# Steps of the triangular inverses moved from VectorE to GpSimd, with a newly planned instruction order

## The chip, the cores and the metric

The kernel runs on one core of one Trainium2 chip. The metric is device time in microseconds (us) for one execution, the median of several. Engines are named as in the profile: PE (TensorE, matmuls; its weight loads are PEld), DVE (VectorE), ACT (ScalarE), POOL (GpSimd), SP (SyncE, which here only issues DMAs).

## What is computed

A linear recurrence over 768 steps for 32 heads (4 batches of 8), and then two dense layers on its output, 3072 tokens of width 320, hidden width 2048:

```
for t in range(S):                                   # S = 768
    y[:, :, t] = einsum('bhd,bhde->bhe', r_t, state)
    Sa = einsum('bhde,bhe->bhd', state, a_t)
    state = state * w_t - outer(Sa, b_t) + outer(v_t, k_t)
...
h = x @ w_in;   x = (h * tanh(softplus(h))) @ w_out          # layer 1
h = x @ w_in2;  x = (h * cos(h)) @ w_out2                    # layer 2
```

All inputs are float32 (the layers' weights are float64 and are split into high and low parts on the chip).

## The kernel before

**The recurrence** is cut into chunks of 32 steps, and the heads into two halves of 16: 2 x 24 = 48 chunks, numbered g = 0 to 47, one after another. Inside a chunk the steps are solved at once with the inverse of a unit triangular matrix of 32 x 32 per head. Each chunk has two parts.

- `pre(g)` needs no state and runs up to seven chunks ahead: two scans on DVE (L570 and L576, tiles PE and RP), four multiplications on DVE (L584 to AM, L590 to KB), two memsets of AM on POOL (L598), the matrices of the chunk on PE (L607), four masked evacuations on DVE (L617, back into AM), transposes (L640). A DMA (L630, L631) writes the triangular part of AM to DRAM (`l_d`).
- `chain(g)` carries the state and so sets the order of chunks: matmuls L782, L805, L796, L854, and two groups L880 at its end, with evacuations between them on ACT (L390, L788) and DVE (L864 to FR, L891 to SV, L899 to Y), and transposes L924 for the next chunk.

**The inverse.** Two chunks form a batch; there are 24, bt = 0 to 23. `inverse(bt)` loads the 2 x 16 matrices' two diagonal blocks of 16 x 16 from `l_d` into tile XM (64 partitions), and inverts them by forward substitution: 14 times a multiplication into XT (L679) and an addition into XM (L677), each on the result of the one before it, 28 steps in all, on 14 to 56 elements per partition. Both inputs of a step lie in SBUF. Then a short memset sets the diagonal (L686), a DMA stores XM to DRAM (`t_d`, L690), another loads it in a new layout to TT (L694), and `halves` joins the blocks: a transpose on DVE (L721), matmuls L716, an operation on DVE (L724), matmuls L718, a copy. TT is what L805 and L796 of the chunk multiply with.

**The dense layers.** Weights are converted on ACT, DVE (L466, L471, L479) and POOL (L508, low parts wil, wol, wix, read from staging tiles H, AU, RL). Layer 1 takes blocks of 256 tokens as the recurrence finishes them: matmuls L983 (16 for each of 8 parts of the hidden width), Mish on ACT (L1053, L1055), the low part of the result on DVE (L1058, tile GL), matmuls L964 (12 for each part). Layer 2 follows when layer 1 is done (L998, L1014, and L983 and L964 for two small blocks), with its low parts on POOL (L1142). There are 1792 matmuls L983 and 1344 L964 in all.

**What sets the order.** Every operation is a task with an engine, a duration in us, predecessors and the buffers it takes. `Plan.run` is a greedy planner: it keeps a clock per engine, starts next the task that can start earliest (small differences are decided by priorities), and writes the instructions in that order. Tasks with `port=True` on DVE and POOL are never planned at the same time. On the chip each engine works off its instructions in the planned order, whatever the real durations are, and waits for semaphores. PE puts matmuls of layer 1 into places where the chain isn't ready. The priorities put the chain first, then `pre` and `inverse` by chunk, then the dense layers.

Of the kernel before, what the change touches and what calls it, by code (L numbers as in the profile page):

```python
# [14 lines left out]
ALU = mybir.AluOpType  # L15
# [23 lines left out]
def bc(ap, shape):  # L39
    return ap.to_broadcast(list(shape))  # L40
# [43 lines left out]
MODE = {"pre.g1": "128x64", "chain.rvz": "128x64", "chain.fmm.f": "128x64", "chain.rhs": "128x32",  # L84
        "chain.zmm": "32x32", "halves.mm.f": "32x32", "chain.stm": "64x128", "chain.ztm": "full"}
LEAVE, CHANGE, ENTER = 0.22, 0.12, 0.13
AGE = 8.0
WAIT = 8.0
SP_SAFE = 1.0

# [161 lines left out]
def body(ctx, tc, ins, out):  # L252
# [141 lines left out]
    def pa(key):  # L394
        return bank[P.at(key)]

    def dve(n, passes=1.0):
        return 0.065 + 0.00104 * n * passes

    def act(n, psum=True, ptr=0):  # L400
        return (0.05 if psum else 0.093) + 0.000833 * n + 0.093 * ptr

    def pool(n):
        return 0.1 + 0.0022 * n
# [7 lines left out]
    INV_LEAD = 32  # L412
    AHEAD_W = 6
    DIRECT = 48
    HV_D, HV_P = (0.36, 0.41), 0.5
    B_HI2 = 1.0
    am_on, GLE = lambda g, d: ("DVE", 0.33), ("DVE",)
    HIE = EITHER
    HIE2, HID2 = ("DVE",), (0.34,)
    LOE2, LOD2 = ("POOL", "DVE"), (pool(512), dve(512))  # L420
# [125 lines left out]
    def fifo(name, t):  # L546
        p = prev_fifo.get(name)
        if p is not None:
            t.preds.append(p)
        prev_fifo[name] = t  # L550
        return t

    def pre(g):
# [16 lines left out]
            V.tensor_tensor_scan(out=pe().rearrange("p q t -> p (q t)"), data0=INv()[:, 768:1032],  # L570
                                 data1=D1.rearrange("p q t -> p (q t)"), initial=0.0, op0=ALU.mult, op1=ALU.add)

        t_sc = fifo("scan", P.add("DVE", 0.62, scan, preds=[t_ld, S_D], acq=[("PE", k("PE"))], prio=pr, port=True))
        def rscan():
            V.reciprocal(out=D1R[:, :, C:], in_=pe()[:, :, C:])
            V.tensor_tensor_scan(out=rp().rearrange("p q t -> p (q t)")[:, ::-1], data0=INv()[:, 769:1033][:, ::-1],  # L576
                                 data1=D1R.rearrange("p q t -> p (q t)")[:, ::-1], initial=0.0,
                                 op0=ALU.mult, op1=ALU.add)

        t_rp = P.add("DVE", 0.85, rscan, preds=[t_sc], acq=[("RP", k("RP"))], prio=pr, port=True)  # L580

        def am_f(p):
            r = slice(64 * p, 64 * p + 40)
# [12 lines left out]
        def az_f(p):  # L596
            r = slice(64 - 64 * p, 128 - 64 * p)
            return lambda: G.memset(am()[r, p], 0.0)  # L598

        t_z0 = P.add("POOL", 0.24, az_f(0), preds=[t_a1], prio=pr)  # L600
        t_z1 = P.add("POOL", 0.24, az_f(1), preds=[t_z0], prio=pr)

        def g1():
            gp = pa(k("G"))[:, 0:256].rearrange("p (q x) -> p q x", x=2 * C)
# [7 lines left out]
        def gev(p, c):  # L612
            r = slice(64 - 64 * p, 128 - 64 * p)

            def f():
                gp = pa(k("G"))[64 * c:64 * c + 64, 0:256].rearrange("r (q p t) -> r p q t", p=2, t=C)
                V.tensor_tensor(out=am()[r, p].rearrange("r (q c) t -> r c q t", c=2)[:, c], in0=gp[:, p],  # L617
                                in1=bc(maskG[r].unsqueeze(1), (64, NQ // 2, C)), op=ALU.mult)
            return f

        t_gl = []
        for c2 in range(2):
            for p in range(2):
                t_gl.append(P.add("DVE", 0.22, gev(p, c2), preds=[t_g], rel=[k("G")], prio=pr))
        Gev[g] = t_gl
        bt, ci = BT_OF[g]
        ld_v = l_d[bt].rearrange("(c q p) j t -> c p j q t", q=NQ, p=2)
# [25 lines left out]
    def inverse(bt):  # L653

        g0, cnt = BATCH[bt]
        pr = -5e3 + (g0 + cnt) * 10 - INV_LEAD
        n = cnt * NU
        rows = lambda: slice(64 * P.at(("X", bt)), 64 * P.at(("X", bt)) + 2 * n)
        x = lambda: XM[rows(), 0:528]
        xu = lambda: XT[rows()]  # L660
        part = lambda h: x()[n * h:n * h + n, 16 - 16 * h:528 - 16 * h]
        blk = lambda: x()[:, 16:528].rearrange("p (j t) -> p j t", t=C)
        dr = lambda d, h: d[bt][:, 16 * h:16 * h + 16].rearrange("n j t -> n (j t)")

        def ld():
            for h in range(2):
                SP.dma_start(part(h), dr(l_d, h))

        t = P.add("SP", 1.0, ld, preds=[ldma[g0 + i] for i in range(cnt)] + [S_X], acq=[("X", ("X", bt))], lat=DMA_LAT, prio=pr)

        def step(i, add):
            w = 15 - i

            def f():
                tv, b = xu()[:, :i * w].rearrange("p (j t) -> p j t", j=i), blk()
                if add:
                    V.tensor_tensor(out=b[:, 0:i, i + 1:16], in0=b[:, 0:i, i + 1:16], in1=tv, op=ALU.add)  # L677
                else:
                    V.tensor_tensor(out=tv, in0=bc(b[:, i:i + 1, i + 1:16], (2 * n, i, w)),  # L679
                                    in1=bc(b[:, 0:i, i:i + 1], (2 * n, i, w)), op=ALU.mult)  # L680
            return f

        for i in range(1, 15):
            for add in range(2):
                t = P.add("DVE", dve(i * (15 - i)), step(i, add), preds=[t], lat=0.13, prio=pr, port=True)
        t = P.add("DVE", 0.1, lambda: V.memset(x()[:, 16:512:33], 1.0), preds=[t], prio=pr)  # L686

        def st():
# [75 lines left out]
    def chain(g):  # L764
# [20 lines left out]
        t = P.add("PE", 0.3, rhs, preds=Gev[g] + [ldma[g], io[g][2]] + (Sev[g - 1] if c else []),  # L785
                  acq=[("PA", k("R"))], rel=[k("AM"), k("SV")], cols=550, prio=pr)
        mated("rhs", c, t)
        t = P.add("ACT", act(160), lambda: A.activation(rs().rearrange("p g d -> p (g d)"), pa(k("R"))[:, 0:160],  # L788
                                                        AF.Copy, scale=-1.0),
                  preds=[t], acq=[("RS", k("RS"))], rel=[k("R")], prio=pr)  # L790

# [80 lines left out]
        ykey = ("Y", hf, yb)

# [456 lines left out]
```

## Time and profile before

| | before |
|---|---|
| median of 3 runs | 1167.32 us (1166.85 to 1177.08) |
| profiled execution | 1172.64 us; its span in the trace is 1170.9 us |
| PE busy | 1047.1 us (89%), 16120 matmul instructions |
| DVE busy | 851.3 us (73%), 2275 instructions |
| ACT busy | 546.0 us (47%) |
| POOL busy | 228.1 us (19%), 278 instructions |
| granted TensorE clock | 0.955 of full speed in the mean |

A float32 matmul of the recurrence appears as two instructions in the trace, so its 16 matmuls of L880 per chunk are 32 there; those of the dense layers appear as one. Times in the trace are counted from the start of the span. Busy PE time is modelled at its ends and overlaps, so it is read together with the counts of matmuls.

### The profile page before, as it was taken

How to read it: one execution, taken by the hardware profiler on the slowest of the kernel's cores; microseconds unless marked ns; L12 is line 12 of the kernel's file. 1: busy time of each engine (PE TensorE's matmuls, PEld its weight loads, DVE VectorE, ACT ScalarE, POOL GpSimd, SP SyncE). 2: the span in 40 equal slices, each digit the busy share in tenths (PEclk: the TensorE clock that was granted, in tenths of full speed). 3: DMA queues.
4: the chain of work that ended last, by engine and by line, in shares of the span. 5: the costliest groups of instructions: out<-in, count | busy, mean ns of one | idle time of the engine just before them, and what ended most of it. 6: DMA issues, size and time to landing. Idle time of an engine off the chain costs nothing. (4 is left out here: it accounts for less than half of the span.)

```text
span 1170.9 us, 39034 instructions
## 1 busy us (share of the span) xinstructions
PE 1047.1 (89%) x16120; PEld 951.9 (81%) x16120; DVE 851.3 (73%) x2275; ACT 546.0 (47%) x1384; POOL 228.1 (19%) x278
## 2 busy tenths in 40 slices
PE   1364988989899988989999999999999999999997
PEld 1353877877787777877888999999999899999997
DVE  8889898879888898788883599433555555555554
ACT  3344464555545555455454444434443444444433
POOL 4223210000000000000000034100333333333333
PEclk9985896989999999999899999999999999999999
DMA  8564345455544555445543354210100000000000
GB/s 236 160 160 144 104 134 156 113 133 142 135 114 129 156 136 156 100 126 134 131 113 89 115 158 138 67 57 26 53 25 1 25 25 26 26 25 12 13 12 23
DMA packets 104913, 112.05 MB, mean 96 GB/s; under 512 B 63520, under 2 KB 84256, under 8 KB 104736
## 3 DMA queue, kind: packets, MB, share of 16 engines
q1 hardware_dynamic: 104736, 109.56, 33.6%
q8 instruction: 127, 2.08, 0.8%
q14 instruction: 50, 0.41, 0.1%
HBM read 91.43 MB, written 18.09 MB: 94 GB/s over the span
## 5 line engine op out<-in xcount | busy, mean ns | idle before, releaser
L1142 POOL TENSOR_TENSOR GL<-H,GH 128x512 fp32r<-128x512 f32 x96 | 124.6, 1298 | 260.6 <-ACT GH L1140 246.4
L390 ACT ACTIVATE FL<-bank 64x160 f32<-64x160 f32 (+1 forms) x376 | 101.7, 295 | 124.3 <-PE bank L924 59.9
L1133 ACT ACTIVATE T<-T,half_pi 128x512 f32<-128x512 f32 x96 | 69.5, 724 | 115.7 <-DVE T L1130 115.7
L1126 DVE TENSOR_SCALAR T<-bank 128x512 f32<-128x512 f32 x96 | 66.4, 692 | 77.6 <-PE bank L998 63.8
L1058 DVE TENSOR_TENSOR GL<-H,GH 128x512 fp32r<-128x512 f32 x96 | 71.4, 744 | 67.6 <-ACT GH L1055 66.6
L1053 ACT ACTIVATE H<-bank 128x512 f32<-128x512 f32 x96 | 57.4, 598 | 119.3 <-PE bank L983 114.4
L1135 DVE TENSOR_TENSOR H<-bank,T 128x512 f32<-128x512 f32 x96 | 66.2, 689 | 56.2 <-ACT T L1133 54.8
L598 POOL MEMSET AM<- 64x256 f32 x96 | 29.4, 306 | 390.9 <-issue 313.3
L607 PE MATMUL bank<-AM,KB 104*64 104x64 f32 x768 | 37.2, 247 | 67.9 <-DVE KB L590 56.9
L983 PE MATMUL bank<-XH,wih 128*128 128x256 f32 x448 | 95.4, 295 | 1.4 <-ACT GH L1055 1.4
L1140 ACT ACTIVATE GH<-H 128x512 fp32r<-128x512 f32 x96 | 60.6, 632 | 72.4 <-DVE H L1135 72.2
L983 PE MATMUL bank<-XL,wih 128*128 128x256 f32 x448 | 91.5, 287 | 0.0
L983 PE MATMUL bank<-XH,wil 128*128 128x256 f32 x448 | 90.5, 284 | 0.4 <-issue 0.4
L607 PEld LDWEIGHTS bank<-AM,KB 104*64 104x64 f32 x768 | 32.0, 158 | 71.2 <-issue 70.3
L880 PE MATMUL bank<-FR,FL 104*64 104x72 f32 x1536 | 72.1, 251 | 16.8 <-issue 8.7
L880 PEld LDWEIGHTS bank<-FR,FL 104*64 104x64 f32 x1536 | 62.8, 155 | 26.1 <-issue 14.6
L983 PEld LDWEIGHTS bank<-XH,wih 128*128 128x128 f32 x448 | 71.0, 194 | 3.4 <-ACT GH L1055 1.5
L679 DVE TENSOR_TENSOR XT<-XM 64x26 f32<-64x26 f32 (+6 forms) x336 | 67.4, 201 | 7.4 <-DMA XM<-l_d 0.3
L677 DVE TENSOR_TENSOR XM<-XM,XT 64x26 f32<-64x26 f32 (+6 forms) x336 | 67.0, 199 | 7.6
L983 PEld LDWEIGHTS bank<-XL,wih 128*128 128x128 f32 x448 | 71.5, 197 | 0.0
L983 PEld LDWEIGHTS bank<-XH,wil 128*128 128x128 f32 x448 | 70.3, 194 | 0.6 <-issue 0.6
L983 PE MATMUL bank<-XH,wix 128*128 128x256 f32 x224 | 69.9, 312 | 0.0
(165 smaller groups left out, 2973.2 us busy)
## 6 DMA issues: line engine op xcount, KB each, us to landing
VR<-in_vR_dram SPq DMA_DIRECT2D x96, 160.0 KB
IN<-in_inT_dram SPq DMA_DIRECT2D x94, 161.4 KB
FR<-in_rI_dram SPq DMA_DIRECT2D x48, 180.0 KB
FR<-in_vF_dram SPq DMA_DIRECT2D x48, 144.0 KB
TMP<-in_w_in_dram SPq DMA_DIRECT2D x12, 512.0 KB
RA<-in_w_in_dram SPq DMA_DIRECT2D x12, 512.0 KB
RA<-in_w_out_dram SPq DMA_DIRECT2D x10, 512.0 KB
SV<-in_vS_dram SPq DMA_DIRECT2D x96, 52.0 KB
```

Source lines behind the costliest of these rows:

```text
L390: A.activation(o, i, AF.Copy)
L607: PE.matmul(gp[c0:c0 + 64, q // 2], kb()[:, q].rearrange("p a t -> p (a t)"), am()[0:104, :, q], start=True, stop=True)
L677: V.tensor_tensor(out=b[:, 0:i, i + 1:16], in0=b[:, 0:i, i + 1:16], in1=tv, op=ALU.add)
L679: V.tensor_tensor(out=tv, in0=bc(b[:, i:i + 1, i + 1:16], (2 * n, i, w)), in1=bc(b[:, 0:i, i:i + 1], (2 * n, i, w)), op=ALU.mult)
L880: PE.matmul(fp[64 * p:64 * p + 64, qp], fl()[0:104, n * D:n * D + 64], fr()[:, n], start=True, stop=True)
L983: PE.matmul(hp[:, f], pss[i][0], pss[i][1], start=(i == 0), stop=(i == 7))
L1058: gl = P.add(GLE, (dve(512),), lambda eng, Hv=Hv, key=key: EN[eng].tensor_tensor(out=GL_t[P.at((key, "gl"))], in0=Hv(), in1=GH_t[P.at((key ...
L1126: a = P.add("DVE", dve(512), lambda f=f, hv=hv, Tv=Tv: V.tensor_scalar(out=Tv(f), in0=hv(), scalar1=0.25, scalar2=MAGIC, op0=ALU.add, op1= ...
L1133: c = P.add("ACT", act(512, False, 1), lambda f=f, Tv=Tv: A.activation(Tv(f), Tv(f), AF.Sin, scale=-TWO_PI, bias=half_pi), preds=[b], aset ...
L1135: gt = P.add("DVE", dve(512), lambda f=f, Tv=Tv, Hv=Hv, hv=hv: V.tensor_tensor(out=Hv(f), in0=hv(), in1=Tv(f), op=ALU.mult), preds=[c, g_f ...
L1140: lambda f=f, Hv=Hv, key=key: A.activation(GH_t[P.at((key, "gh"))], Hv(f), AF.Copy),
L1142: gl = P.add("POOL", pool(512), lambda f=f, Hv=Hv, key=key: G.tensor_tensor(out=GL_t[P.at((key, "gl"))], in0=Hv(f), in1=GH_t[P.at((key, "g ...
```

## The change

For batches 1 to 23 the 28 steps and the memset of the diagonal are POOL's (`G`) in place of DVE's (`V`); batch 0 keeps DVE. The planner's duration of such a step on POOL is 0.1 us plus 0.0022 us per element, with 0.1 us until the next; that of a step on DVE is set to 0.165 us. A dozen other durations that the planner uses are set anew, most of them upward (scan, multiplications, evacuations on ACT and DVE), and `AGE`, a waiting time in its rule for PE, goes from 8 to 4 us. No other instruction is added, removed or changed in shape. The numbers set the order alone.

```
-AGE = 8.0
+AGE = 4.0
...
-        t_sc = fifo("scan", P.add("DVE", 0.62, scan, preds=[t_ld, S_D], acq=[("PE", k("PE"))], prio=pr, port=True))
+        t_sc = fifo("scan", P.add("DVE", 0.64, scan, preds=[t_ld, S_D], acq=[("PE", k("PE"))], prio=pr, port=True))
...
+        own = bt >= 1
+        IE = G if own else V
+
         def step(i, add):
...
                 if add:
-                    V.tensor_tensor(out=b[:, 0:i, i + 1:16], in0=b[:, 0:i, i + 1:16], in1=tv, op=ALU.add)
+                    IE.tensor_tensor(out=b[:, 0:i, i + 1:16], in0=b[:, 0:i, i + 1:16], in1=tv, op=ALU.add)
                 else:
-                    V.tensor_tensor(out=tv, in0=bc(b[:, i:i + 1, i + 1:16], (2 * n, i, w)),
+                    IE.tensor_tensor(out=tv, in0=bc(b[:, i:i + 1, i + 1:16], (2 * n, i, w)),
                                     in1=bc(b[:, 0:i, i:i + 1], (2 * n, i, w)), op=ALU.mult)
...
-                t = P.add("DVE", dve(i * (15 - i)), step(i, add), preds=[t], lat=0.13, prio=pr, port=True)
-        t = P.add("DVE", 0.1, lambda: V.memset(x()[:, 16:512:33], 1.0), preds=[t], prio=pr)
+                t = P.add("POOL" if own else "DVE", 0.1 + 0.0022 * i * (15 - i) if own else 0.165, step(i, add), preds=[t], lat=0.1 if own else 0.04, prio=pr, port=True)
+        t = P.add("POOL" if own else "DVE", 0.1, lambda: IE.memset(x()[:, 16:512:33], 1.0), preds=[t], prio=pr)
```

Line numbers behind the change are higher by three from L677 on (L679 becomes L682, L880 becomes L883, L983 becomes L986).

The first place is on DVE, early, where the work ahead for chunk 5 is done (AM_206 is its AM, XM and XT are the inverse's tiles). Before, the steps of batch 1 stand in it:

```order
L576 SCALAR_TENSOR_TENSOR RP_215<-IN_192,D1R 104x264
L584 TENSOR_TENSOR AM_206<-IN_192,PE_199 40x256
L679 TENSOR_TENSOR XT<-XM 64x14
L677 TENSOR_TENSOR XM<-XM,XT 64x14
L679 TENSOR_TENSOR XT<-XM 64x26
L677 TENSOR_TENSOR XM<-XM,XT 64x2x13
```

Now the same place reads:

```order
L576 SCALAR_TENSOR_TENSOR RP_215<-IN_192,D1R 104x264
L584 TENSOR_TENSOR AM_206<-IN_192,PE_199 40x256
L617 TENSOR_TENSOR AM_205<-bank_145,maskG 64x4x32 x4
L590 TENSOR_TENSOR KB_217<-IN_192,RP_215 104x8x32
L466 TENSOR_SCALAR H_178<-H_178 128x512
```

The 28 steps between the two are gone from DVE, and the evacuation for chunk 4 (AM_205) and the weights' conversion follow directly.

The second place is on POOL at the same point of the program (wil, wix and wol are low parts of weights, AM_205 to AM_207 are AM of chunks 4 to 6, AM_202 that of chunk 8). Before:

```order
L598 MEMSET AM_205 64x256 x2
L508 TENSOR_TENSOR wil_165<-H_177,wih_164 128x512
L508 TENSOR_TENSOR wil_165<-H_178,wih_164 128x512
L598 MEMSET AM_206 64x256 x2
L598 MEMSET AM_207 64x256 x2
L508 TENSOR_TENSOR wix_166<-H_179,GH_181 64x512
```

Now the two batches' steps, 56 in all with memsets of AM between them, stand ahead of the same subtractions; these are the last of batch 2 and the first of batch 3:

```order
L682 TENSOR_TENSOR XT<-XM 64x14
L680 TENSOR_TENSOR XM<-XM,XT 64x14
L689 MEMSET XM 64x16
L508 TENSOR_TENSOR wil_165<-H_177,wih_164 128x512
L508 TENSOR_TENSOR wil_165<-H_178,wih_164 128x512
L508 TENSOR_TENSOR wix_166<-H_179,GH_181 64x512
L508 TENSOR_TENSOR wol1a<-H_177,woh1a 128x512
L508 TENSOR_TENSOR wol1a<-H_178,woh1a 128x512
L508 TENSOR_TENSOR wil_165<-H_179,wih_164 128x512
L598 MEMSET AM_202 64x256 x2
L682 TENSOR_TENSOR XT<-XM 64x14
```

The subtractions for the weights moved behind the inverses of batches 1 and 2.

The third place is on PE at chunk 4 (AM_205; TT_232 is the inverse of its batch). Before, its first matmuls L782 are followed by work ahead and then by dense matmuls of layer 1:

```order
L782 MATMUL bank_147<-SV_218,AM_205 32x40 x16
L607 MATMUL bank_144<-AM_202,KB_217 64x64 x8
L640 MATMUL bank_146<-ident,KB_217 128x104 x4
L607 MATMUL bank_145<-AM_203,KB_217 64x64 x8
L983 MATMUL bank_148<-XH_185,wih_164 128x256 x2
L983 MATMUL bank_148<-XH_185,wil_165 128x256 x2
```

Now chunk 4 runs to its end without a dense matmul, and chunk 5 begins (AM_206):

```order
L808 MATMUL bank_147<-TT_232,RS_233 40x32 x2
L799 MATMUL bank_146<-RS_233,TT_232 32x40 x16
L857 MATMUL bank_145<-VR_221 64x64 x8
L883 MATMUL bank_147<-FR_219,FL_212 64x72 x8
L883 MATMUL bank_146<-FR_219,FL_212 64x72 x8
L927 MATMUL bank_144<-ident,SV_218 104x40 x4
L927 MATMUL bank_145<-ident,SV_218 104x40 x4
L785 MATMUL bank_147<-SV_218,AM_206 32x40 x16
```

The dense matmuls that stood ahead of the rest of chunk 4 moved behind chunk 5.

## Rows read from the trace of the kernel before

**Rows 1.** Page, part 2: PE and DVE, busy tenths in 40 slices.
```profile
PE   1364988989899988989999999999999999999997
DVE  8889898879888898788883599433555555555554
```

**Rows 2.** Line L880 around the ends of chunks 0, 3, 6, 47: durations, first and last start.
```profile
L880 PE MATMUL bank<-FR,FL x21: 324/327/328, 60.7 to 61.9; 104*64 104x72 f32 x21
...
L880 PE MATMUL bank<-FR,FL x32: 327/328/380, 99.5 to 101.3; 104*64 104x72 f32 x32
...
L880 PE MATMUL bank<-FR,FL x32: 226/226/277, 167.3 to 168.3; 104*64 104x72 f32 x32
...
L880 PE MATMUL bank<-FR,FL x32: 226/226/277, 653.9 to 654.9; 104*64 104x72 f32 x32
```

**Rows 3.** Stretches: us, then PE, PEld, DVE, ACT, POOL busy, PEclk, DMA share, GB/s.
```profile
62.20:101.60 39.40, 26.75 (x645) 22.93 (x644) 34.59 (x104) 22.62 (x65) 13.19 (x11) 0.72 0.57 158
101.60:146.00 44.40, 30.60 (x537) 27.82 (x539) 39.92 (x133) 19.12 (x51) 8.42 (x14) 0.75 0.44 120
168.60:655.20 486.60, 441.64 (x10690) 388.99 (x10691) 401.15 (x1361) 251.94 (x795) 20.84 (x68) 0.94 0.47 126
655.20:1170.90 515.70, 508.81 (x3299) 479.08 (x3299) 300.89 (x463) 216.05 (x375) 159.06 (x118) 1.00 0.15 47
```

**Rows 4.** The last two stretches, L964 alone, then L983: PE, PEld busy (count).
```profile
168.60:655.20 486.60, 112.27 (x574) 88.62 (x575) 0.94 0.47 126
655.20:1170.90 515.70, 112.24 (x699) 103.12 (x699) 1.00 0.15 47
...
168.60:655.20 486.60, 121.06 (x760) 103.46 (x760) 0.94 0.47 126
655.20:1170.90 515.70, 116.12 (x928) 112.29 (x928) 1.00 0.15 47
```

**Rows 5.** Chain that ended last, 659 to 667 us: start, length, line.
```profile
659.88 3.51 PE bank L964 x24
663.40 3.65 PE bank L983 x32
```

**Rows 6.** Page, part 5: inverse steps on DVE, busy us, mean ns, idle before.
```profile
L679 DVE TENSOR_TENSOR XT<-XM 64x26 f32<-64x26 f32 (+6 forms) x336 | 67.4, 201 | 7.4 <-DMA XM<-l_d 0.3
L677 DVE TENSOR_TENSOR XM<-XM,XT 64x26 f32<-64x26 f32 (+6 forms) x336 | 67.0, 199 | 7.6
```

**Rows 7.** Two stretches of two chunks: all engines, then L964, then L983.
```profile
344.80:366.60 21.80, 21.80 (x666) 19.58 (x666) 17.70 (x52) 13.80 (x41) 1.23 (x4) 1.00 0.51 144
420.00:444.40 24.40, 20.01 (x547) 17.30 (x551) 21.61 (x78) 12.68 (x40) 1.23 (x4) 1.00 0.54 142
...
344.80:366.60 21.80, 4.06 (x24) 3.54 (x24) 1.00 0.51 144
420.00:444.40 24.40, 3.95 (x18) 2.67 (x18) 1.00 0.54 142
...
344.80:366.60 21.80, 6.71 (x44) 5.51 (x44) 1.00 0.51 144
420.00:444.40 24.40, 5.14 (x36) 4.49 (x36) 1.00 0.54 142
```

**Rows 8.** POOL in order of time: start, length, instruction, idle before it.
```profile
25.30 1.27 POOL L508 TENSOR_TENSOR wol1a<-H,woh1a 128x512 fp32r<-128x512 f32 x1 [4.14 <-ACT woh1a L390]
...
142.60 0.73 POOL L508 TENSOR_TENSOR wol1b<-RL,woh1b 128x256 fp32r<-128x256 f32 x1 [1.15 <-ACT woh1b L390]
143.40 0.67 POOL L598 MEMSET AM<- 64x256 f32 x2
```

**Rows 9.** POOL and DVE around 106 us; then L584 from 168.6 to 623.6.
```profile
106.01 1.29 POOL L508 TENSOR_TENSOR wix<-H,GH 64x512 fp32r<-64x512 f32 x1 [5.39 <-DVE XT L679]
...
106.21 1.37 DVE L584 TENSOR_TENSOR AM<-IN,PE 40x256 f32<-40x256 f32 x1
...
L584 DVE TENSOR_TENSOR AM<-IN,PE 40x256 f32<-40x256 f32 x70 | 29.2, 417 | 1.0
```

**Rows 10.** DVE's waits before 655.2 us: us in total, times, longest.
```profile
DVE TA L721 <- DMA TT<-t_d: 2.7, 3, 1.7
```

More of the change, by code (lines that the diff above doesn't have):

```diff
@@ L400, in act @@
     def act(n, psum=True, ptr=0):
-        return (0.05 if psum else 0.093) + 0.000833 * n + 0.093 * ptr
+        return (0.08 if psum else 0.123) + 0.000833 * n + 0.093 * ptr
     def pool(n):
@@ L414, in body @@
     DIRECT = 48
-    HV_D, HV_P = (0.36, 0.41), 0.5
+    HV_D, HV_P = (0.4, 0.43), 0.52
     B_HI2 = 1.0
-    am_on, GLE = lambda g, d: ("DVE", 0.33), ("DVE",)
+    am_on, GLE = lambda g, d: ("DVE", 0.385), ("DVE",)
     HIE = EITHER
@@ L578, in rscan @@
                                  op0=ALU.mult, op1=ALU.add)
-        t_rp = P.add("DVE", 0.85, rscan, preds=[t_sc], acq=[("RP", k("RP"))], prio=pr, port=True)
+        t_rp = P.add("DVE", 0.91, rscan, preds=[t_sc], acq=[("RP", k("RP"))], prio=pr, port=True)
         def am_f(p):
@@ L598, in az_f @@
             return lambda: G.memset(am()[r, p], 0.0)
-        t_z0 = P.add("POOL", 0.24, az_f(0), preds=[t_a1], prio=pr)
-        t_z1 = P.add("POOL", 0.24, az_f(1), preds=[t_z0], prio=pr)
+        t_z0 = P.add("POOL", 0.31, az_f(0), preds=[t_a1], prio=pr)
+        t_z1 = P.add("POOL", 0.31, az_f(1), preds=[t_z0], prio=pr)
         def g1():
@@ L623, in pre @@
             for p in range(2):
-                t_gl.append(P.add("DVE", 0.22, gev(p, c2), preds=[t_g], rel=[k("G")], prio=pr))
+                t_gl.append(P.add("DVE", 0.27, gev(p, c2), preds=[t_g], rel=[k("G")], prio=pr))
         Gev[g] = t_gl
@@ L787, in chain @@
         mated("rhs", c, t)
-        t = P.add("ACT", act(160), lambda: A.activation(rs().rearrange("p g d -> p (g d)"), pa(k("R"))[:, 0:160],
+        t = P.add("ACT", 0.29, lambda: A.activation(rs().rearrange("p g d -> p (g d)"), pa(k("R"))[:, 0:160],
                                                         AF.Copy, scale=-1.0),
@@ L869, in chain @@
         for h in range(2):
-            ve[h] = P.add("DVE", 0.36, rve(h), preds=[r0] + z[2 * h:2 * h + 2] + [ve[i] for i in range(h)], rel=[k("V")], prio=pr)
+            ve[h] = P.add("DVE", 0.41, rve(h), preds=[r0] + z[2 * h:2 * h + 2] + [ve[i] for i in range(h)], rel=[k("V")], prio=pr)
         yb, yc = divmod(c, 4)
@@ L910, in chain @@
             if not last:
-                s = [P.add("DVE", 0.34, sev(h, p), preds=[ft, io[nx][2]], prio=pr) for p in range(2)]
+                s = [P.add("DVE", 0.315, sev(h, p), preds=[ft, io[nx][2]], prio=pr) for p in range(2)]
             sevs += s
@@ L914, in chain @@
             y_acq = [("Y", ykey)] if (yc == 0 and h == 0) else []
-            yevs.append(P.add("DVE", dve(128), yev(h), preds=[ft] + s + yevs, acq=y_acq, rel=rel, prio=pr + 1))
+            yevs.append(P.add("DVE", 0.26, yev(h), preds=[ft] + s + yevs, acq=y_acq, rel=rel, prio=pr + 1))
         Sev[g] = sevs
```

## Prediction

> **What bounds the kernel now.** I first read the forty slices of the page [rows 1]. They show two regimes: DVE stands at eight or nine tenths for the first 26 slices and at five after them, while PE rises to nine and stays there to the end. So I looked for the place where the recurrence ends. The groups of L880 (one pair per chunk of the recurrence, 48 chunks) give it [rows 2]: chunk 0 ends near 62.2 us, chunk 3 near 101.6, chunk 6 near 168.6, the last one, chunk 47, near 655.2 (last start plus its length, rounded). The stretches between these points [rows 3] are the table to keep in mind. From 655.2 to 1170.9 PE is busy 508.81 of 515.70 us at a granted clock of 1.00, that is 2.4 GHz: matmuls of the two dense layers back to back. That part gets shorter only if fewer matmuls are left for it. Before 655.2 PE also looks busy (441.64 of 486.60), but DVE is at 401.15 of 486.60 there, nearly full as well.
>
> How much of PE's time before 655.2 is the dense layers? Back to back, 24 matmuls of L964 take 3.51 us and 32 of L983 take 3.65 [rows 5]: 0.1463 and 0.1141 us each. Between 168.6 and 655.2 there are 574 and 760 of them [rows 4], worth 84.0 + 86.7 = 170.7 us. The other 315.9 us belong to the 41 chunks 7 to 47: **7.70 us per chunk** for the recurrence's own matmuls and every wait. This is the term that the change can move.
>
> The trace holds an experiment on it. Two stretches of two chunks each differ in how many inverse steps DVE ran in them: 344.8 to 366.6 with 52 DVE instructions, and 420.0 to 444.4 with 78, where the additional ones are steps [rows 7]. With the dense matmuls taken out (24 and 44 in the first, 18 and 36 in the second, 8.53 and 6.74 us), a chunk costs (21.80 - 8.53)/2 = 6.63 us where DVE is free of steps and (24.40 - 6.74)/2 = 8.83 where it is not. In the first PE is busy for the whole stretch, in the second 20.01 of 24.40. So DVE holds up the chunks, and PE is close behind it.
>
> **What is removed from DVE.** 23 batches of 28 steps, 644 of 672, at about 0.20 us [rows 6]: 129 us, and 23 short memsets. Per chunk that is 14 steps, 2.8 us. Nothing else of DVE's work changes. As an order the change shows twice on PE. Counted in the two orders up to chunk 47's last L880, 864 L983 and 645 L964 stand ahead of it before, and 812 and 600 now (the first pair is the trace's: 1792 - 928 and 1344 - 699 [rows 4]). And ahead of chunk 6's, 104 and 72 stood, now 32 and 0: chunks 4 to 6 no longer wait behind dense matmuls for their inverse.
>
> **The sum, in four terms.**
> (1) End of chunk 6. Before, chunks 1 to 3 took 39.4/3 = 13.1 us each [rows 3], at a clock of 0.72 and, by the order, with 27 steps on DVE, and chunk 4 alone took 44.4 us, with DVE busy 39.92 of them. Now six chunks follow one another. I take 13.1 less 27 x 0.20/3 = 1.8 us for the steps, plus 32 dense matmuls at half clock (32 x 0.228 = 7.3 us, 1.2 per chunk): 12.5 us. Chunk 0 is unchanged at 62.2 (DVE has as much ahead of it as before), so chunk 6 ends at 62.2 + 6 x 12.5 = 137.2 us in place of 168.6. Bounds: adding up DVE's rows ahead of that point gives 40 us less than before, hence 128.6; with 13.1 us and the 7.3 on top, 148.
> (2) Dense matmuls inside chunks 7 to 47: 780 x 0.1141 + 600 x 0.1463 = 176.8 us.
> (3) 41 chunks at x us. Upper bound: 7.70, nothing gained. Lower bound: 6.6, the free stretch (with the last three chunks, which hold no work ahead, a little under). I take 6.95, nearer the lower end, since every chunk now has no steps on DVE. The 0.35 above 6.6 is for what GpSimd gives back (below) and for the clock, 1.00 in that stretch and 0.94 in the mean [rows 3, 7]. 41 x 6.95 = 285.0.
> (4) After chunk 47: 515.7 us and the matmuls that slid behind it, 52 x 0.1141 + 45 x 0.1463 = 12.5: 528.2.
> Sum: 137.2 + 176.8 + 285.0 + 528.2 = 1127.2 us of span against 1170.9, 43.7 us less. The profiled execution took 1172.64 us and the median of the runs is 1167.32, 5.3 lower; 43.7 less than the median is **1124 us**.
>
> **What GpSimd pays.** No step of this shape ran there. The nearest rows are its subtractions: 1.27 us for 512 elements and 0.73 for 256 [rows 8], so 0.0021 us per element above 0.19. A step has 14 to 56 elements, 40 in the mean: 0.28 us. Instructions behind one another start 0.07 us after the last end (0.73 from 142.60, next 143.40): 0.35 per step, 28 steps 9.8 us, and two pairs of memsets of 0.67 us. That is 11.1 us in the 22.5 us that two chunks last, so GpSimd has room. Bounds: 0.20, as on DVE, and, for a step that each time waits out a whole multiplication of DVE, 0.35 + 0.42 = 0.77 us [rows 8, 9]; GpSimd itself would be the bound from (22.5 - 1.34)/28 = 0.76 on. I take 0.35 to 0.45.
> The steps issue no DMA, but the store of the finished inverse on SP now waits for GpSimd, and behind it stand the loads of IN and VR and the next XM load. On GpSimd itself the steps stand ahead of the wil subtractions, so the weights of the first layer come later; dense matmuls begin only behind chunk 5, which covers it. Were that cover gone, six subtractions and 56 steps, some 20 us, would be late, but only for dense matmuls, and PE would still fill that time with chunks.
>
> **The lock.** At 106.01 us GpSimd began a subtraction of 1.29 us; a DVE multiplication begun 0.2 us later ended with it, and took 1.37 us instead of 0.42 [rows 9]. So an instruction of DVE with two inputs in SBUF waits until GpSimd's is done. With steps of 0.28 us it waits 0.14 in the mean. A chunk has seven such (two scans, four multiplications, a GL), and GpSimd is in steps nearly half the time: 7 x 0.45 x 0.14 = 0.4 us per chunk. That is 16% of the 2.8 us saved, 0.17 of the 1.07 us between 7.70 and 6.63; the rest of the 0.35 is clock.
>
> **The rivals.**
> A, PE was the bound already. For it: PE busy 441.64 of 486.60. Against it: the two stretches above. Then x stays 7.70, and the sum is 137.2 + 176.8 + 315.7 + 528.2 = 1157.9, by the same subtraction 1154.
> B, the lock takes back most of what is saved. If each of the seven instructions waits for a whole step, 7 x 0.28 = 2.0 of the 2.8 us are lost; x is 7.70 - 1.07 x 0.8/2.8 = 7.39, the sum 1145.2, a run 1142. For it: the row at 106.21 waited out its whole rival. Against it: that rival was five times as long as a step, and a step must begin just ahead of every such instruction.
> The Trainium skill has this as a warning: Perfetto Trace Analysis, section Optimizing Scalar/DVE Operations, says that the two engines share a read port and that offloading between them might not help; SBUF — State Buffer, section SBUF: two separate sides, calls it an exclusive lock, held for the whole instruction. On the lock the trace agrees (1.37 us beside 1.29); where it leaves nothing of the gain, the time would be A's.
> C, the inverse comes late (the one that is slower). DVE is in order and transposes TT (L721) as soon as its row is reached; before, it waited 2.7 us in all for that [rows 10]. Between the last masked evacuation of a batch and its L721 there stand 20 to 40 us of DVE rows in the new order, fewer than before (22 to 46), and in that time the matrix goes out and back through DRAM twice and through 28 steps, 9.8 us without the lock. Where this runs over, SV and FR behind it wait, and so do the chunks. At 3 us per batch, 23 batches give 69: 1196 of span, a run 1193. It decides from 43.7/23 = 1.9 us per batch. Against it: DVE's rows won't be back to back any more, so those 20 to 40 us last longer.
>
> **How the numbers follow.** The forecast has 0.72, A 0.10, B 0.10, C 0.08. The predicted time is the forecast's, 1124. Its own lower end takes both lower bounds: 128.6 + 176.8 + 41 x 6.55 + 528.2 = 1102, a run of 1098; with x another 0.15 lower through the new order, 1092. The upper end reaches over A: 1158. C is left outside. About 1% (11.7 us) is what a measurement can tell from no change: faster holds the forecast, B and a little of A, 0.83, since 1154 lies close to 1155.6; within it, 0.09, the rest of A; slower, 0.08, C.
>
> **What would show it.** Right: the last L880 ends at 590 to 605 us, the dense matmuls after it number 980 and 744, DVE falls by some 125 us, the interval 101.6 to 146 has no counterpart, and XM/XT steps on GpSimd take 0.25 to 0.35 us. Wrong: L584 0.2 us or more above 0.42 (B), waits of DVE L721 for TT above 40 us (C), or chunks of 12 us with PE full (A). A step of over 0.76 us on GpSimd would make that engine the bound.

## The result and the profile after

The changed kernel takes **1118.86 us** in the median (1112.02 to 1127.88, four runs) against 1167.09 before. The ratio is 0.957 with a 95% interval of 0.948 to 0.966, so it is 3.4 to 5.2% faster. The forecast was 1124, with a range of 1092 to 1158. The profiled execution is the slowest of the four, 1127.88 us with a span of 1126.2; compared with the profiled execution before (1172.64) it is 44.8 us shorter.

The page of the kernel after, engine sums and then the slices (against [rows 1]):

```profile
PE 1042.0 (93%) x16120; PEld 947.5 (84%) x16120; DVE 743.1 (66%) x1607; ACT 545.3 (48%) x1385; POOL 448.2 (40%) x945
...
PE   2388899999999998989999999999999999999997
...
DVE  8978689677666676768445994325555656565553
...
POOL 5465567635634445335301451002333333333333
```

PE now stands at eight or nine from the third slice on, and DVE mostly at six to eight where it stood at eight and nine. POOL, nearly empty in the middle before (20.84 us busy in the long stretch of [rows 3]), is at about half. The end of the recurrence is read as in [rows 2], by the groups of the last line of a chunk, now L883, at chunks 6 and 47:

```profile
L883 PE MATMUL bank<-FR,FL x32: 327/328/379, 134.4 to 136.3; 104*64 104x72 f32 x32
...
L883 PE MATMUL bank<-FR,FL x32: 226/226/277, 596.9 to 597.9; 104*64 104x72 f32 x32
```

Chunk 6 ends 32 us earlier than before and chunk 47 57 us earlier. The stretches, in the columns of [rows 3]: chunks 1 to 6 (from before's 62.2 us; chunk 0 ends at 65.1 here), 7 to 47, and what follows; then the same for L967 (before L964) and L986 (before L983) alone, as in [rows 4]:

```profile
62.20:136.20 74.00, 62.13 (x1479) 54.00 (x1480) 58.20 (x145) 40.34 (x124) 46.38 (x111) 0.97 0.55 147
136.20:597.70 461.50, 439.62 (x10886) 386.64 (x10884) 325.03 (x849) 261.97 (x824) 207.31 (x631) 0.96 0.51 139
597.70:1126.20 528.50, 521.52 (x3410) 491.86 (x3405) 305.87 (x468) 220.80 (x383) 160.53 (x118) 1.00 0.15 46
...
136.20:597.70 461.50, 119.40 (x600) 93.64 (x600) 0.96 0.51 139
597.70:1126.20 528.50, 119.93 (x744) 109.87 (x744) 1.00 0.15 46
...
136.20:597.70 461.50, 118.68 (x780) 100.12 (x780) 0.96 0.51 139
597.70:1126.20 528.50, 123.47 (x980) 118.97 (x980) 1.00 0.15 46
```

In the middle stretch DVE is busy 325.03 of 461.50 us (70%, before 82%), PE 95% (before 91%). With the dense matmuls taken out at the rates of [rows 5], a chunk costs (461.5 - 780 x 0.1141 - 600 x 0.1463)/41 = 6.94 us, where it cost 7.70. I call this number x below, as the prediction did.

The steps themselves on POOL: the page's groups (busy us, mean ns, idle before them), then one of the two lines with its shortest, median and longest duration:

```profile
L682 POOL TENSOR_TENSOR XT<-XM 64x14 f32<-64x14 f32 (+6 forms) x322 | 111.8, 347 | 199.4 <-DMA XM<-l_d 176.7
L680 POOL TENSOR_TENSOR XM<-XM,XT 64x14 f32<-64x14 f32 (+6 forms) x322 | 107.6, 334 | 24.1
...
L682 POOL TENSOR_TENSOR XT<-XM x322: 205/282/2791, 44.6 to 555.2; 64x14 f32<-64x14 f32 x23, 64x36 f32<-64x36 f32 x23, 64x50 f32<-64x50 f32 x23, 64x56 f32<-64x56 f32 x23
```

The median is the 0.28 us that was forecast, the mean is 0.34: 97 of the 644 steps last over 0.5 us. Most of the idle time before them, 176.7 of 199.4 us, is waiting for XM to arrive from DRAM, so POOL works in bursts of one batch. DVE's own work in chunks 7 to 47 (busy us, mean ns):

```profile
L584 DVE TENSOR_TENSOR AM<-IN,PE 40x256 f32<-40x256 f32 x70 | 29.6, 423 | 0.5
L590 DVE TENSOR_TENSOR KB<-IN,RP 104x256 f32<-104x256 f32 x70 | 29.3, 422 | 6.1 <-PE bank L640 5.5
L576 DVE TENSOR_TENSOR_SCAN RP<-IN,D1R 104x264 f32<-104x264 f32 x35 | 26.5, 758 | 1.2
L570 DVE TENSOR_TENSOR_SCAN PE<-IN,D 104x264 f32<-104x264 f32 x35 | 25.6, 732 | 0.6
```

Before, the same four lines had means of 417, 419, 708 and 705 ns. What the steps have to do with the difference is seen from the same lines in e4 (below), which has the order of after without the steps:

```profile
L584 DVE TENSOR_TENSOR AM<-IN,PE 40x256 f32<-40x256 f32 x70 | 29.6, 423 | 0.5
L590 DVE TENSOR_TENSOR KB<-IN,RP 104x256 f32<-104x256 f32 x70 | 28.9, 417 | 3.5 <-PE bank L640 2.9 <-issue 0.2
L576 DVE TENSOR_TENSOR_SCAN RP<-IN,D1R 104x264 f32<-104x264 f32 x35 | 25.5, 729 | 1.2
L570 DVE TENSOR_TENSOR_SCAN PE<-IN,D 104x264 f32<-104x264 f32 x35 | 25.0, 715 | 0.6
```

So 0 to 29 ns per instruction go with the steps; the rest is there without them. DVE hardly waits for the steps on POOL. And of the inverse's late arrival, all of DVE's waits for TT ahead of 640 us come to this (total, times, longest):

```profile
DVE TA L724 <- DMA TT<-t_d: 6.0, 5, 3.5
```

### The profile page after: what moved, and what is told of

Read it like the earlier page. It is cut to its first block, busy times and chain, and to the rows that moved or that the text cites. A ratio compares the mean times of both kernels' runs of the same rounds, so it can differ in the third digit from the quotient of the medians.

```text
span 1126.2 us, 38994 instructions
## 1 busy us (share of the span) xinstructions
PE 1042.0 (93%) x16120; PEld 947.5 (84%) x16120; DVE 743.1 (66%) x1607; ACT 545.3 (48%) x1385; POOL 448.2 (40%) x945
## 4 chain that ended last, share of the span: by engine, by line
PE 43%; issue 8%; DVE 4%; POOL 3%; DMA 2%; ACT 1%; SPq 0%; POOLq 0%; DVEq 0%; ACTq 0%
PE bank L986 10%; PE bank L967 10%; PE bank L1001 8%; PE bank L1017 8%; POOL GL L1145 3%; PE bank L883 1%; DVE GL L1061 1%; DMA TT<-t_d 1%; DVE AU L479 1%; PE bank L1106 1%; PE bank L857 1%; DVE AU L471 1%; PE bank L808 1%; PE bank L799 1%; PE bank L785 0%
## 5 line engine op out<-in xcount | busy, mean ns | idle before, releaser
L682 POOL TENSOR_TENSOR XT<-XM 64x14 f32<-64x14 f32 (+6 forms) x322 | 111.8, 347 | 199.4 <-DMA XM<-l_d 176.7
L1061 DVE TENSOR_TENSOR GL<-H,GH 128x512 fp32r<-128x512 f32 x96 | 73.1, 762 | 83.1 <-ACT GH L1058 82.5
L680 POOL TENSOR_TENSOR XM<-XM,XT 64x14 f32<-64x14 f32 (+6 forms) x322 | 107.6, 334 | 24.1
L986 PE MATMUL bank<-XH,wih 128*128 128x256 f32 x448 | 95.6, 295 | 0.0
L986 PE MATMUL bank<-XL,wih 128*128 128x256 f32 x448 | 89.7, 282 | 0.3 <-issue 0.3
L986 PE MATMUL bank<-XH,wil 128*128 128x256 f32 x448 | 89.5, 282 | 0.0
L883 PE MATMUL bank<-FR,FL 104*64 104x72 f32 x1536 | 69.7, 247 | 8.7 <-issue 3.7
L607 PE MATMUL bank<-AM,KB 104*64 104x64 f32 x768 | 38.2, 252 | 42.2 <-DVE KB L590 30.7
L867 DVE TENSOR_TENSOR FR<-bank,maskR 64x256 f32<-64x256 f32 x96 | 40.3, 420 | 53.9 <-PE bank L857 24.5
L883 PEld LDWEIGHTS bank<-FR,FL 104*64 104x64 f32 x1536 | 60.4, 152 | 17.3 <-issue 7.2
L894 DVE TENSOR_TENSOR SV<-bank,PE 40x160 f32<-40x160 f32 x184 | 59.2, 322 | 20.6 <-PE bank L883 14.9
L986 PEld LDWEIGHTS bank<-XH,wih 128*128 128x128 f32 x448 | 69.7, 191 | 2.9
L986 PEld LDWEIGHTS bank<-XL,wih 128*128 128x128 f32 x448 | 69.9, 192 | 0.4 <-issue 0.4
L607 PEld LDWEIGHTS bank<-AM,KB 104*64 104x64 f32 x768 | 32.9, 164 | 44.3 <-issue 27.0
L986 PEld LDWEIGHTS bank<-XH,wil 128*128 128x128 f32 x448 | 69.3, 191 | 0.0
```

What stands on the lines that cost most here:

```text
L607: PE.matmul(gp[c0:c0 + 64, q // 2], kb()[:, q].rearrange("p a t -> p (a t)"), am()[0:104, :, q], start=True, stop=True)
L680: IE.tensor_tensor(out=b[:, 0:i, i + 1:16], in0=b[:, 0:i, i + 1:16], in1=tv, op=ALU.add)
L682: IE.tensor_tensor(out=tv, in0=bc(b[:, i:i + 1, i + 1:16], (2 * n, i, w)), in1=bc(b[:, 0:i, i:i + 1], (2 * n, i, w)), op=ALU.mult)
L883: PE.matmul(fp[64 * p:64 * p + 64, qp], fl()[0:104, n * D:n * D + 64], fr()[:, n], start=True, stop=True)
L986: PE.matmul(hp[:, f], pss[i][0], pss[i][1], start=(i == 0), stop=(i == 7))
L1061: gl = P.add(GLE, (dve(512),), lambda eng, Hv=Hv, key=key: EN[eng].tensor_tensor(out=GL_t[P.at((key, "gl"))], in0=Hv(), in1=GH_t[P.at((key ...
```

## The experiments

All of them are timed beside the kernel before, and "ratio" is to that kernel on the same chip. In the table, c6 and c47 are the ends of chunks 6 and 47 in the profiled execution, and x is worked out as above with the dense matmuls that each order has there. Since the orders differ in how many these are, it is x and not c47 that can be compared from row to row. The ends are read to within 0.5 us: the last record of after's chunk 6, shown above, ends at 136.3 + 0.33 = 136.6. This moves x by 0.01 at most.

| run | steps of batches 1 to 23 | median us | ratio (95%) | c6 | c47 | x |
|---|---|---|---|---|---|---|
| before | DVE | 1167.09 | 1 | 168.6 | 655.2 | 7.70 |
| after | POOL | 1118.86 | 0.957 (0.948 to 0.966) | 136.2 | 597.7 | 6.94 |
| e1_numbers_only | DVE | 1150.16 | 0.988 (0.984 to 0.992) | 158.7 | 638.0 | 7.15 |
| e2_pool_old_numbers | POOL | 1119.83 | 0.960 (0.953 to 0.967) | 134.9 | 561.6 | 6.54 |
| e6_before_no_steps | none | 1115.62 | 0.959 (0.955 to 0.963) | 154.8 | 598.5 | 6.66 |
| e4_after_no_steps | none | 1106.75 | 0.952 (0.948 to 0.955) | 134.2 | 577.0 | 6.48 |
| e5_memset_steps | memsets on POOL | 1109.10 | 0.950 (0.946 to 0.954) | 134.4 | 582.0 | 6.60 |
| e9_mult_twice | POOL, 42 per batch | 1173.58 | 1.004 (1.002 to 1.006) | 144.9 | 640.0 | 7.76 |
| e3_half | half each | 1120.47 | 0.962 (0.956 to 0.967) | 131.5 | 594.2 | 6.81 |
| e13_measured_half | half each | 1133.10 | 0.970 (0.966 to 0.975) | 138.8 | 635.6 | 6.89 |
| e12_measured_thirds | 2/3 POOL | 1125.15 | 0.963 (0.958 to 0.969) | 146.3 | 638.3 | 6.74 |
| e10_pool_measured | POOL | 1111.22 | 0.953 (0.949 to 0.956) | 135.2 | 600.5 | 6.51 |
| e11_tie | POOL | 1107.30 | 0.947 (0.942 to 0.953) | 136.6 | 578.1 | 6.58 |
| e14_measured_tie | POOL | 1106.30 | 0.948 (0.943 to 0.952) | 136.7 | 604.8 | 6.46 |

**The two halves of the change, apart.** The change moves steps and sets numbers anew. One run takes the new numbers and leaves the steps on DVE, the other moves the steps and keeps the old numbers.

```
e1:  -        own = bt >= 1
     +        own = False
e2:  -AGE = 4.0
     +AGE = 8.0
     (and every other duration of the planner as before, but for that of a step on POOL)
```

> All the new planner numbers, but the steps of every batch stay on VectorE. If the gain comes from taking 129 us of steps off VectorE (the forecast), this stays near before: 1150 to 1175 us, chunks at about 7.7 us beside the dense matmuls. If the gain comes from planning with durations from the trace, it is near after: 1115 to 1130 us.

> Steps of batches 1 to 23 on GpSimd (planned there as in after), every other planner number as before, AGE 8. By the forecast most of the gain is here: 1115 to 1135 us. If the new numbers carry it: 1150 to 1170 us.

The numbers alone bring 1.2%, the move alone 4.0%, both together 4.3%. The move carries the gain; the two do not add up (they would give 5.2%). Each of these kernels is one order, and another draw of after's order moves the time by 1.0% (below), so the 1.2% is not shown to be the numbers' doing. The chunks of e1 cost 7.15 us, not the 7.7 expected. Between e1 and after, which have the same numbers, x falls by 0.21 us only, 8.6 us over 41 chunks, while chunk 6 ends 22 us earlier: in this pair most of the gain lies ahead of chunk 7.

**Is it the place on DVE that the steps cost?** If PE is the bound (rival A), taking the steps out altogether gains little. If the lock takes much back (rival B), an order without steps is much faster than one with steps on POOL. e6 leaves them out in the order of before, e4 in the order of after.

```
e6:      def f():
    +        if bt >= 1:
    +            return
e4:      def f():
    +        if own:
    +            return
```

> The order of before, with the steps of batches 1 to 23 left out on VectorE (not computed). By the forecast VectorE held the chunks: 41 chunks at 6.6 to 6.9 us and a shorter stall at chunk 4, 1105 to 1130 us. If PE was the bound already (rival A): 1150 us or more.

> The order of after, with the 644 steps left out of GpSimd's instructions (so the inverses of batches 1 to 23 are not computed; everything else runs in the same order). By the forecast GpSimd gives back about 0.2 us per chunk through the lock: some 7 us, so 1105 to 1115 us. If the lock takes back 2.0 of 2.8 us per chunk (rival B) the steps cost about 30 us: 1085 to 1095 us. If late inverses hold the chunks (rival C), the waits for TT vanish and it gains 20 us or more.

With nothing but the steps gone, the order of before takes 4.1% less. Its stretch from chunk 7 to 47 is 443.7 us instead of 486.6, with the same matmuls in it:

```profile
154.80:598.50 443.70, 424.10 (x10697) 376.43 (x10691) 310.46 (x834) 251.28 (x796) 20.78 (x68) 0.96 0.50 138
598.50:1114.20 515.70, 508.85 (x3305) 479.05 (x3299) 300.89 (x463) 215.99 (x375) 158.94 (x118) 1.00 0.15 47
```

So A falls: PE was not the bound. Its busy time of 441.64 us at a clock of 0.94 [rows 3] is 424.10 us here, at 0.96, for the same matmuls. The end stretch is 515.7 us to the tenth, as before, which confirms that nothing happens to it unless matmuls slide behind chunk 47. B falls too: the whole distance between after and its own order without steps is 12.1 us in the medians, 0.6% by the ratios.

**What these 12 us are.** They can be POOL being occupied, or the lock. In e5 each step is replaced by a memset of 280 elements, which reads no tile and lasts 0.33 us.

```
         def f():
+            if own:
+                G.memset(XM[rows(), 16:16 + 280], 0.0)
+                return
```

> The order of after; in place of each of the 644 steps GpSimd writes zeros into 280 columns of XM, about as long (0.3 us) but without reading SBUF (the inverses of batches 1 to 23 are not computed). Without steps at all this order took 1107 us, with them 1119. If those 12 us are the lock on the shared port, this is near 1107 (1103 to 1111). If they are GpSimd's time, steps that end late, it is near after: 1114 to 1124.

Chunks 7 to 47 without steps (e4), then with memsets in their place (e5):

```profile
134.20:577.00 442.80, 429.65 (x10888) 378.40 (x10883) 323.07 (x850) 263.14 (x826) 33.68 (x97) 0.98 0.52 146
...
134.40:582.00 447.60, 430.50 (x10891) 379.02 (x10888) 323.68 (x851) 264.13 (x827) 205.80 (x631) 0.98 0.53 144
```

POOL is as busy as in after (205.80 against 207.31 us, 631 instructions in both), and the time is that of e4. So the occupancy of POOL costs at most 2 to 5 us; what after has on top of it, 9.8 us in the medians, goes with steps that read SBUF, which points to the lock. The size of it is not settled: by the ratios it is 0.75%, the interval of after is 0.9% to either side, and its four runs reach from 1112 to 1128 us. With the old numbers, e2 and e6 lie 4.2 us apart, but they do not share an order (701 and 537 dense matmuls in chunks 7 to 47 against 760 and 574).

That there is a lock the two traces do show. Of after's 644 steps 222 run beside a DVE instruction of the scans, the multiplications, L1061, L1043, L471 or L479, which read two inputs from SBUF; they last 0.49 us in the mean, the other 422 last 0.26. Of e5's memsets 299 run beside such an instruction and 345 do not, and both last 0.33.

**How much room the inverse has on POOL.** Rival C did not come about, but is it near? e9 does each multiplication of a batch twice, which makes 42 instructions of 28.

```
+                  for _ in range(2 if own else 1):
                     IE.tensor_tensor(out=tv, in0=bc(b[:, i:i + 1, i + 1:16], (2 * n, i, w)),
```

> The order of after; each multiplication of a step on GpSimd is issued twice (same result), so 42 instructions per batch in place of 28. At 0.46 us from start to start, as after shows, a batch's chain is 6.4 us longer, 19 us in all, still under the 22 us of two chunks. By the forecast GpSimd has room: 1115 to 1135 us. If the leads ahead of L724 are used up (rival C), each of 23 batches loses up to 6.4 us: 1160 to 1260 us.

14 more instructions at 0.36 us, start to start, are 5 us per batch (from the first to the last step a batch takes 17.9 us in the median, in after 12.1), and all of the gain is gone: 1.004. The middle stretch, and the waits ahead of 640 us that have grown (total, times, longest):

```profile
144.90:640.00 495.10, 452.00 (x10883) 397.64 (x10882) 325.84 (x850) 262.51 (x825) 288.54 (x898) 0.92 0.48 130
...
PE bank L607 <- POOL AM L598: 25.3, 10, 4.6
DVE TA L725 <- DMA TT<-t_d: 16.6, 6, 6.4
```

In after the first of these is 0.5 us and the second 6.0. So two things are late when a batch is late. DVE stands still for TT, as C had it. And the memsets of AM, which stand behind the steps in POOL's order, hold up PE's L607; the prediction had not named this one. The two waits grew by 25.3 - 0.5 + 16.6 - 6.0 = 35 us. The two profiled executions, to which these waits belong, are 42.2 us apart, 33.6 of them in chunks 7 to 47. Waits of two engines can fall into the same time, so the 35 us are no full account of it. By the ratios e9 lies 54.5 us above after (1.0039 - 0.9572 of the 1167.5 us that before took on that chip). That is outside what room on GpSimd would have given, and inside what was expected of rival C. The occupancy is no warning here: POOL is busy 288.54 of 495.10 us, 58%.

**A dose.** If DVE's place is what costs, half the batches on POOL should give half.

```
e3:  +        own = bt >= 1 and bt % 2 == 1
e13: +        own = bt >= 1 and bt % 2 == 1      (with the duration of e10, below)
e12: +        own = bt >= 1 and bt % 3 != 0      (with the duration of e10)
```

> After's numbers, but only the odd batches (12 of 23) on GpSimd, the even ones on VectorE, planned so. With all on VectorE the new numbers took 1150 us, with all on GpSimd 1119. If the gain goes with VectorE's load: 1130 to 1142 us. If chunks are held by single late inverses on VectorE, half of the batches are enough to keep nearly all of the stalls: 1142 to 1152.

> As e12_measured_thirds with every second batch on VectorE. By the first reading 1104 to 1112 us; by the second 1110 to 1118.

> GpSimd's step at its traced length, and every third batch on VectorE. Half of the batches on GpSimd was as good as all of them (1120 against 1119 us). If GpSimd's chain and VectorE's load both cost a little, a mixture is best: 1102 to 1108 us. If PE is the bound by now: 1108 to 1114, like the 1111 with all batches on GpSimd.

With none, half, two thirds and all of the batches on POOL, the new numbers give 1150; 1120 or 1133; 1125; and 1106 to 1119. The direction is that of a dose, and no mixture beats the whole move. But e3 alone, level with after, contradicts its own forecast, e12 and e13 are 11 us or more above both of theirs, and by x no dose shows (6.81, 6.89 and 6.74 for the mixtures, 6.94 for after, 6.46 to 6.58 for three more orders with all batches on POOL). The two kernels with half differ by 13 us with the same steps on the same engines. Only the order differs between them. How much an order alone does had to be measured.

**What an order alone does.** After plans a step on POOL with 0.1 + 0.0022 us per element; the trace has 0.28 us at 40 elements and 0.36 from start to start. e10 plans with the length seen. e11 changes only TIE, a number by which the planner varies each duration by up to 1% at random, and e14 does both.

```
e10: -  t = P.add("POOL" if own else "DVE", 0.1 + 0.0022 * i * (15 - i) if own else 0.165, ...
     +  t = P.add("POOL" if own else "DVE", 0.25 + 0.0021 * i * (15 - i) if own else 0.165, ...
e11: -TIE = 97
     +TIE = 98
e14: both
```

> After, with the planner's duration of a step on GpSimd at 0.25 us plus 0.0021 us per element (0.33 us in the mean, as the trace of after shows, 0.19 in after). Were late inverses the rest of the loss, planning with the true length gives back some of the 12 us between after and the order without steps: 1108 to 1114 us. If it is the lock or chance in the order: 1115 to 1125.

> After with another seed for the planner's tie-breaking noise (TIE 98 in place of 97; it scatters the durations by up to 1%). The work is the same. If after's 1119 us is typical of its numbers: 1112 to 1125 us. If single orders scatter more than the differences read so far: outside of that.

> The kernel with GpSimd's step planned at its traced length (1111 us), with the seed 98 as well. If the true length is what helps, it stays below e11_tie by about 8 us; if the 8 us were the luck of one order, the two are alike.

e10 alone looked like a gain of half a per cent. e11 shows that another draw of the same planner gives 1107.3 with the old length, 1% below after by the ratios, and e14 that the length adds nothing to it. So a better duration is not shown to help, and an order of this planner has to be taken as one draw: two draws lie 5 us apart with the one duration (e10, e14) and 12 with the other (after, e11). After is the slower of its two, and e11 and e14 are faster than both given kernels. The scatter also bounds what the small differences above can mean: those between before, e1 or e9 and the kernels without DVE's steps are larger than it, those between e3, e12, e13, e10 and after, or between before and e1, are hardly so. Before against e6, and after against e4 and e5, have one order in both.

## Why the prediction was right, step by step

**The four terms.** (1) Chunk 6 ends at 136.6 us (137.2). (2) The dense matmuls in chunks 7 to 47 are 780 and 600, as read from the order. (3) x is 6.94 (6.95). (4) The end stretch is 528.1 us (528.2). The sum holds to 1 us, the difference between the profiled executions is 44.8 us (43.7), and between the medians 48.2. The main reason, that DVE's place holds up the chunks, which the two stretches of [rows 7] had shown within one trace, is confirmed by e6: in the order of before the steps alone are worth 4.1%. Its x of 6.66 is the 6.63 of the free stretch; that it is so to 0.03 is chance in part, since five steps still stood in that stretch and its clock was 1.00, not 0.96.

Part of the closeness is luck. The profiled execution is the slowest of the four, 9 us above the median, at a granted clock of 0.979, where the two fastest runs had 0.992. If the whole difference lies in chunks 7 to 47, the median run has an x of about 6.94 - 9.0/41 = 6.7. And another draw of the order would have given 1107. The range held these as well.

**Term 1 is right by two errors that cancel.** It let chunk 0 end at 62.2 us as before, and gave six chunks 12.5 us each: 13.1 us at a clock of 0.72, less 1.8 for the steps, plus 1.2 for dense matmuls at half clock. Chunk 0 ends at 65.1 us, 2.9 later, and the six chunks take 71.5 us, 11.9 each. The first error goes with the planner's numbers: chunk 0 ends at 64.8 to 66.6 us in every order with the new ones and at 61.5 to 63.3 with the old ones. The second, 0.6 us per chunk too many, does not come from the clock, 0.72 there and 0.96 now. Here are the six chunks in after, e11 and e14, and the last line of chunk 4 in e11 and e14:

```profile
65.10:136.60 71.50, 60.27 (x1453) 52.39 (x1455) 56.67 (x141) 40.15 (x123) 45.46 (x107) 0.96 0.55 148
65.00:136.70 71.70, 61.54 (x1572) 54.31 (x1572) 59.01 (x144) 44.89 (x131) 46.23 (x109) 1.00 0.58 153
65.40:136.80 71.40, 58.43 (x1448) 51.06 (x1448) 51.82 (x131) 39.27 (x122) 42.12 (x105) 0.64 0.55 149
...
L883 PE MATMUL bank<-FR,FL x32: 327/328/381, 107.8 to 109.7; 104*64 104x72 f32 x32
...
L883 PE MATMUL bank<-FR,FL x32: 327/328/380, 107.6 to 109.5; 104*64 104x72 f32 x32
```

The six chunks take the same time at a granted clock of 1.00 and of 0.64, and the chain's matmul lasts 327 ns in chunk 4 of e11, at 1.00, as in chunk 4 of e14, at 0.50. So a granted clock of 0.72 does not by itself make such a chunk dearer. In the order of before without steps (e6) chunks 1 to 3 take 11.8 us each, so the steps are most of what stood between the 13.1 and that. The steps' new place costs little: e4, without steps, needs 69.2 us for the six. What does set the 11.9 us I did not find. The long wait did go, as forecast: chunk 4 took 44.4 us before [rows 3], and the longest interval between the ends of two chunks is 17.2 us now, at chunk 12. It went with the order: e6, which only leaves the steps out of the order of before, still takes 36.5 us for chunk 4, and e2 takes 11.0.

**What DVE is rid of.** 129 us were forecast, some 125 of them to be seen, and DVE's busy time fell by 108 (851.3 to 743.1). It isn't the lock that took the rest: e4, with no step anywhere, has 742.1. The 0.20 us of [rows 6] is the length of one record, and records of neighbours overlap. DVE before, in order of time:

```profile
108.08 0.20 DVE L677 TENSOR_TENSOR XM<-XM,XT 64x44 f32<-64x44 f32 x1
108.20 0.42 DVE L584 TENSOR_TENSOR AM<-IN,PE 40x256 f32<-40x256 f32 x1
108.54 0.21 DVE L679 TENSOR_TENSOR XT<-XM 64x50 f32<-64x50 f32 x1
```

The multiplication starts 0.12 us after a step that lasts 0.20, and the next step 0.08 us before the multiplication's end. So 667 instructions freed 109 us, 0.164 us each, 2.3 us per chunk rather than 2.8. The gain per chunk did not hang on this, since it was taken from the two stretches.

**The cost on POOL.** Right for the single step (0.28 in the median) and its pitch (0.36 in the median, 0.35 forecast), wrong for the batch: from the first to the last, 28 steps take 10 to 14 us in 20 of 23 batches and 17 to 26 in the other three, rather than 9.8, and some steps are far longer than the median.

**The lock, on the wrong engine.** The prediction let DVE wait 0.4 us per chunk for POOL. By the four lines in after and e4, the steps make the scans 17 and 29 ns longer and the multiplications 0 and 5 ns, so a chunk loses some 0.05 us there. (In [rows 9] the multiplication also did not end with the subtraction, as the prediction read it, but 0.28 us behind it.) It is POOL that waits: 644 steps with a mean 0.06 us above the median are some 39 us. Two places in order of time, POOL and DVE together:

```profile
163.63 0.75 DVE L471 SCALAR_TENSOR_TENSOR RL<-RL 128x256 uint32<-128x256 uint32 x2
163.80 2.79 POOL L682 TENSOR_TENSOR XT<-XM 64x14 f32<-64x14 f32 x1 [1.21 <-DMA XM<-l_d]
164.31 0.75 DVE L479 SCALAR_TENSOR_TENSOR RL<-RL 128x256 uint32<-128x256 uint32 x2
164.98 0.70 DVE L570 TENSOR_TENSOR_SCAN PE<-IN,D 104x264 f32<-104x264 f32 x1
165.59 0.93 DVE L1043 TENSOR_TENSOR XL<-XR,XH 128x768 fp32r<-128x768 f32 x1
...
214.46 0.29 POOL L682 TENSOR_TENSOR XT<-XM 64x56 f32<-64x56 f32 x1
...
214.72 0.71 DVE L570 TENSOR_TENSOR_SCAN PE<-IN,D 104x264 f32<-104x264 f32 x1
214.83 1.33 POOL L680 TENSOR_TENSOR XM<-XM,XT 64x56 f32<-64x56 f32 x1
215.34 0.67 DVE L1061 TENSOR_TENSOR GL<-H,GH 128x512 fp32r<-128x512 f32 x1
```

The smallest step, 14 elements, takes 2.79 us, from within one DVE instruction to the end of the last of a run of them (165.59 + 0.93 = 166.52; the step ends at 166.59). The second waits out a scan and the GL behind it. The cost to the whole came out near what was allowed for it, some 10 us by e5 (with the doubt named there) where 41 x 0.17 = 7 had been put into x. That it reaches the time through a later inverse is what is left when DVE loses so little; no run shows that path by itself.

**The rivals.** A is refuted by e6 and e4, B by the four DVE lines and e4. The warning of the Trainium skill (Perfetto Trace Analysis, section Optimizing Scalar/DVE Operations), that moving work between these two engines might not help, does not hold here: the lock is real, and 4% is gained nevertheless. C did not occur: TT is waited for 6.0 us in all instead of 2.7 [rows 10], far under its 43.7. But the argument that kept it small was weak. The prediction saw room on POOL because a batch of 11.1 us fits into 22.5, and put the limit at 0.76 us per step. e9 takes 17.9 us per batch in the median, inside the 28 x 0.76 = 21.3 us of that limit, and loses everything. The limit is how soon the inverse, and the memsets behind it, are needed, and not how much of POOL's time is taken; 5 to 6 us more per batch is beyond it. Not all of that reaches the time: e9's 54.5 us above after are 2.4 per batch, where C's sum put its turning point at 1.9.

**What stays open.** Whether the new numbers bring anything by themselves beyond the scatter of orders, what sets the time of chunks 1 to 6, the size of the lock's cost beyond "up to some 10 us", and what makes one draw of the order better than another.

## What to carry to other kernels

Where two stretches of one trace differ in the presence of the work that is to be moved, their difference is a better price than the sum of that work's durations: it gave 6.63 us per chunk, and the order without the work ran at 6.66. Before moving a dependent chain to an idle engine, compare the chain's length, and that of whatever stands behind it in the new engine's order, with the time until its result is needed, not the engine's free share. And where a planner sets the order, run a second draw of the same plan before reading a per cent into a change of its numbers.

## What the runs showed of the hardware

A GpSimd instruction that reads SBUF does not only wait for the DVE instruction that it meets, but can wait for every one of a run of DVE instructions behind one another: 0.28 us became 2.79 beside four such lines. Of the 97 steps over 0.5 us in after, 95 end 3 to 170 ns behind the end of a DVE instruction with two inputs in SBUF. DVE's own four lines lost 0 to 29 ns to the steps. A DVE instruction can be passed over as well, by longer work on GpSimd. Right behind the step of 2.79 us, two subtractions on GpSimd held up a scan that lasts 0.71 us elsewhere:

```profile
166.56 1.41 POOL L508 TENSOR_TENSOR wol1b<-RL,woh1b 128x256 fp32r<-128x256 f32 x2
...
166.67 1.87 DVE L576 TENSOR_TENSOR_SCAN RP<-IN,D1R 104x264 f32<-104x264 f32 x1
```

The Trainium skill (SBUF — State Buffer, section SBUF: two separate sides) says that whichever of the two starts first holds the shared pair for its whole instruction. Here the engine that waits is also passed over by the next instruction of the other one, if that is ready. The same section says that a DVE instruction with two inputs in SBUF contends only with a GpSimd instruction that reads SBUF; the memsets of e5 agree, with 0.33 us in the mean beside such DVE instructions and without them.

A matmul's record does not always follow the granted clock: that of the chain's matmul L883 lasted 327 ns in chunk 4 at a granted clock of 1.00 (2.4 GHz) in e11 and at 0.50 (1.2 GHz) in e14, and 226 ns in chunk 47 of after. Why, no run here shows.
